# Side products behind the second product, and an expert's split weights kept on chip, in a fused attention and mixture-of-experts kernel

## The chip, the core and the metric

The kernel runs on one core of a Trainium2 chip. TensorE (PE) multiplies, VectorE (DVE), ScalarE (ACT) and GpSimd (POOL) work elementwise, SyncE (SP) issues the transfers between main memory and the chip's buffers. Each engine runs its own instructions strictly in the order in which they stand, and engines wait for each other by semaphores. The metric is the device time of one execution in microseconds.

## The reference

Eight batches of eight heads go through an attention with 32 memory slots; its output, 4608 rows of 512, goes through four experts whose results are summed with normalised weights.

```python
a = exp(phi - max(phi)); a = a / (sum(a) + 1e-9)          # over 576 positions
k_m, v_m = a^T k, a^T v                                   # 32 slots per head
scores = q k_m^T / 8
attn = softmax(scores)                                    # over the 32 slots
x = attn v_m                                              # 4608 x 512 after the transpose
out = 0
for e in range(4):
    h = max(x @ w1[e], 0)                                 # 512 -> 1024
    out += p[:, e:e + 1] * (h @ w2[e])                    # 1024 -> 512
```

## The kernel before

**Numbers in two halves.** Most float32 operands are written as a rounded high part (an ACT copy to a narrower form) and the remainder (a DVE subtraction), and a product is three matmuls: high by high, high by low, low by high. `split` (L149) is that pair of instructions.

**Folding the attention into the expert.** x is never made. For each expert, v_m is multiplied with w1 once (`vw_mm`, L398), which gives a small matrix `vw`, and the softmax weights `AT` are multiplied with `vw`.

**Steps.** The batches are taken in four pairs, with four experts each; a pair and an expert make 32 steps, 512 steps in all: two batches (`odd`), two halves of their columns, and eight blocks j of 128 hidden units. For a step s there are

- the **first product** `first_mm(s)` (L449): six matmuls over 256 or 320 columns into a PSUM bank, tile `p1`;
- `first_hi` (L462, ACT) and `first_lo` (L477, DVE): the split of max(p1, 0) into `h` (and, where 320 columns are done, `hm`);
- the **second product** `second(s)` (L487): six or nine matmuls over 512 columns that add into the banks `p2`; at j = 7 DVE adds them to the output (L513, L515).

The first product runs AHEAD = 2 steps before its second product. PSUM has eight banks: four for `p2`, and four (`pm`) that `p1` shares with all other products. A new tile in `pm` waits until the bank's last reader is done.

**Side work.** Everything that prepares later steps is side work: splitting weights (`plan_w1`, `plan_w2`), the attention of the next batches (`plan_att`), and the products v_m by w1. The last come in two sorts: for the first pair of batches with all of w1 split anew (`plan_vw`: L401 to L403, read by ACT at L413 and DVE at L419), for later ones from split halves that the first pair stored in main memory (`keep_w1`, L142) and that are loaded again (`plan_vw_heads`: L708 splits nothing, it converts what was loaded; L712 multiplies; L720 copies out; L730 moves rows; L766, L770 and L774 add and split them). A planner (`schedule`, L600) assigns each such operation to a step; the side products are those on PE: L401 to L403, L712, the attention's L265 and L268, L1028, L1163 and L857.

**Order inside a step.** From step 18 on (`MANUAL`) `run_step` (L1235) writes the order out. On PE it is: first product of step s + 2, side products, second product of step s. On DVE the step's side operations are cut in two (`cut`, L1226): those that fit a limit of 2300 (a planner's cost, 290 + 2.42 per column; nothing at j = 0) and wait for no other engine of the same step go ahead of `first_lo`, the others behind it. On ACT a limit of 1400 does the same around `first_hi`.

**Steps 0 to 17** are given by tables (`UNITS_1`, `W1_1`, `VW_1`, `REST_0`) and ordered by a scheduler. Batch 0 needs the first expert's w1 first. It is split as eight tiles, in the head of the kernel and in step 1. In steps 10 to 13 `W1_1` has the same four pieces of w1 loaded and split once more, for batch 1, and `unit_w1(..., True)` stores each of these tiles in main memory as it is made. `new_w1` (L136) hands out six buffers in turn: two named `w1`, four named `rows`.

```python
        n = w1n[0] % (2 + RB)
        w1n[0] += 1
        tag = {"tag": "w1", "bufs": 2} if n < 2 else {"tag": "rows", "bufs": RB}
```

Of the kernel before, what the change touches and what calls it, by code (L numbers as in the profile page):

```python
# [10 lines left out]
F32R = mybir.dt.float32r  # L11
# [7 lines left out]
P = 128  # L19
# [4 lines left out]
NJ = F // P  # L24
# [15 lines left out]
RB = 4  # L40
# [5 lines left out]
STEADY = tuple(range(0, 26))  # L46

UNITS_1 = (1, 5, 5, 6, 5, 6, 8, 9, 10, 11, 11, 12, 17, 13, 13, 20)
W1_1 = (10, 10, 12, 13)
VW_1 = (11, 12, 12, 13, 15, 15, 16, 17)  # L50

REST_0 = (2, 1, 6, 6, 1, 1, 1, 1, 5, 1, 2, 1, 2)
# [3 lines left out]
def body(ctx: ExitStack, tc: tile.TileContext, qm, qt, qh, kv, kvt, phi, phn, prob, w1, w2, out):  # L56
    nc = tc.nc
    pool = lambda name, **k: ctx.enter_context(tc.tile_pool(name=name, bufs=1, **k))
    const, wp, work, att = pool("const"), pool("wp"), pool("work"), pool("att")
# [63 lines left out]
    def take_key(key):  # L123
        assert order[count[1]] == key and count[1] in staged, (key, count)
        raws[key] = staged.pop(count[1])
        count[1] += 1

    def free_key(key):
        del raws[key]
        released.add(numbers[key])  # L130
        stage_released()


    w1t, w2t, w1n = {}, {}, [0]

    def new_w1():  # L136
        n = w1n[0] % (2 + RB)
        w1n[0] += 1
        tag = {"tag": "w1", "bufs": 2} if n < 2 else {"tag": "rows", "bufs": RB}
        return wp.tile([P, 2, 512], F32R, name="w1", **tag)  # L140

    def keep_w1(e, fh, hp):  # L142
        for i in range(2):
            nc.sync.dma_start(
                kept[e, fh, hp][i].rearrange("(s r) f -> r s f", s=2),
                w1t[fh, hp][64 * i:64 * i + 64].bitcast(F32),
            )
# [5 lines left out]
    def split_w1(raw, fh, hp, eng):  # L153
        t = new_w1()
        split(t, raw[:, hp % 2, :], eng)
        w1t[fh, hp] = t

    def unit_w1(k, e, fh, g, keep=False):
        def emit(raw):
            for i in range(2):  # L160
                split_w1(raw, fh, 2 * g + i, nc.vector)
                if keep:
                    keep_w1(e, fh, 2 * g + i)
        return ("w1", e, fh, g), emit

    def unit_w2(k, e, j2, eng=nc.vector):
# [269 lines left out]
    def vw_unit(k, e, fh, hp, odds, tag):  # L436
        vw_out(vw_mm(k, fh, hp, tag), k * E + e, fh, hp, odds)
# [4 lines left out]
    def where(s):  # L442
        k, s = divmod(s, PAIR)
        e, s = divmod(s, STEPS)
        odd, s = divmod(s, 2 * NJ)
        half, j = divmod(s, NJ)
        return k, e, odd, half, j

    def first_mm(s):  # L449
        k, e, odd, half, j = where(s)  # L450
        at_t = st["AT", 2 * k + odd]
        n = HALF[odd][half]
        ps = psum.tile([P, 512], F32, name="p1", tag="pm", bufs=4)[:, :n]
        c, f = slice(HALF[odd][0] * half, HALF[odd][0] * half + n), slice((j % 4) * P, (j % 4) * P + P)
        for g in range(2):
            w = vw[k * E + e, odd, j // 4, g]
            nc.tensor.matmul(ps, w[:, 0, f], at_t[:, g, 0, c], start=g == 0, stop=False)  # L457
            nc.tensor.matmul(ps, w[:, 0, f], at_t[:, g, 1, c], start=False, stop=False)  # L458
            nc.tensor.matmul(ps, w[:, 1, f], at_t[:, g, 0, c], start=False, stop=g == 1)  # L459
        return ps  # L460

    def first_hi(s, ps):  # L462
        _, _, odd, _, j = where(s)
        h = work.tile([P, 2, 2 * P], F32R, name="h", tag="h", bufs=AHEAD + 2)
        parts = [(h, slice(0, 2 * P), slice(0, 2 * P))]
        if ps.shape[1] == WIDE:
            if odd == 0:
                mid[j] = work.tile([P, 2, P], F32R, name="hm", tag="hm", bufs=NJ)
                parts.append((mid[j], slice(0, 64), slice(2 * P, WIDE)))
            else:  # L470
                parts = [(mid[j], slice(64, P), slice(0, 64)), (h, slice(0, 2 * P), slice(64, WIDE))]
        for t, to, at_ in parts:
            nc.scalar.activation(t[:, 0, to], ps[:, at_], AF.Relu)  # L473
        hs[s] = h
        return parts

    def first_lo(ps, parts):  # L477
        for t, to, at_ in parts:
            nc.vector.scalar_tensor_tensor(  # L479
                t[:, 1, to], ps[:, at_], 0.0, t[:, 0, to].bitcast(F32), ALU.max, ALU.subtract  # L480
            )
# [5 lines left out]
    def second(s):  # L487
        k, e, odd, half, j = where(s)
        h = hs.pop(s)
        w = w2t[k, e, j]  # L490
        t0 = (0, 2, 5, 7)[2 * odd + half]
        left = [(t0 + i, h[:, :, i * P:i * P + P]) for i in range(2)]
        if t0 == 5:
            left.append((4, mid[j]))
        for t, x in left:
            if j == 0:
                po[t] = psum.tile([P, DM], F32, name="p2", tag="p2", bufs=4)
            nc.tensor.matmul(po[t], x[:, 0, :], w[:, 0, :], start=j == 0, stop=False)  # L498
            nc.tensor.matmul(po[t], x[:, 0, :], w[:, 1, :], start=False, stop=False)  # L499
            nc.tensor.matmul(po[t], x[:, 1, :], w[:, 0, :], start=False, stop=j == NJ - 1)  # L500
        if j < NJ - 1:
            return
        if e == 0:
            a = work.tile([P, 1024], F32, name="acc", tag="acc", bufs=4)
            for i in range(2):
                acc[k, t0 + i] = a[:, i * DM:i * DM + DM]
            if t0 == 5:
                acc[k, 4] = work.tile([P, DM], F32, name="accm", tag="accm", bufs=1)
        for t, _ in left:
            a, n = acc[k, t], TP * k + t  # L510
            p = pt[:, n, e:e + 1]
            if e == 0:
                nc.vector.tensor_scalar_mul(a, po[t], p)  # L513
            else:
                nc.vector.scalar_tensor_tensor(a, po[t], p, a, ALU.mult, ALU.add)  # L515
            if e == E - 1:
                nc.sync.dma_start(out[n * P:n * P + P, :], a)
# [4 lines left out]
    def at(s, unit):  # L522
        plan[s].append(unit if isinstance(unit, tuple) else (None, unit))
# [9 lines left out]
    def vw_at(s, *a):  # L533
        at(s, lambda: vw_unit(*a, ("pm", 4)))

    rest = [unit_scores(0, t0) for t0 in (2, 4)] + [lambda t0=t0: transposes(0, t0) for t0 in (2, 4)]
    rest += [unit_w1(0, 0, 1, g) for g in range(2)]
    rest += [unit_w2(0, 0, j2) for j2 in range(1, 4)]
    rest += [lambda hp=hp: vw_unit(0, 0, 1, hp, (0,), ("pm", 4)) for hp in range(NP)]
# [5 lines left out]
        at(UNITS_1[1 + i], u)  # L545
    for fh in range(2):
        for g in range(2):
            at(W1_1[2 * fh + g], unit_w1(0, 0, fh, g, True))
            for i in range(2):
                vw_at(VW_1[4 * fh + 2 * g + i], 0, 0, fh, 2 * g + i, (1,))  # L550
    class Op:
        def __init__(self, eng, cost, fn, deps, lo=0, take=None, free=None, late=None):
# [666 lines left out]
    def emit(op):  # L1219
        if op.take is not None:  # L1220
            take_key(op.take)
        op.fn()
        if op.free is not None:
            free_key(op.free)

    def cut(ops_, limit, s):  # L1226
        n = 0
        for op in ops_:
            limit -= op.cost
            if limit < 0 or any(d.step == s and d.eng != op.eng for d, _ in op.deps):  # L1230
                break
            n += 1
        return ops_[:n], ops_[n:]

    def run_step(s):  # L1235
        todo_s, ahead = todo[s], s + AHEAD < LAST
        run_plan(s)
        for op in todo_s["SP"]:
            emit(op)
        if ahead:  # L1240
            ps = first_mm(s + AHEAD)
        before, after = cut(todo_s["ACT"], 1400, s)
        for op in before:
            emit(op)
        if ahead:
            parts = first_hi(s + AHEAD, ps)
        for op in after + todo_s["POOL"]:
            emit(op)
        before, after = cut(todo_s["DVE"], 2300 if s % NJ else 0, s)
        for op in before:  # L1250
            emit(op)
        if ahead:
            first_lo(ps, parts)
        for op in after + todo_s["PE"]:
            emit(op)
        second(s)


    order += early
# [5 lines left out]
    def run_plan(s):  # L1265
        for key, emit in plan[s]:
            if key is None:
                emit()
            else:
                emit(take())  # L1270
# [100 lines left out]
    with tc.manual_schedule():  # L1371
        for s in range(MANUAL, LAST):
            run_step(s)
# [40 lines left out]
```

## Time and profile before

| what | value |
|---|---|
| median of three runs | 1382.89 us (1382.28 to 1385.92) |
| the profiled execution | 1383.84 us, of which the span from first to last instruction is 1382.0 us |
| granted TensorE clock, mean | 0.996 |
| DMA | 211.51 MB in 102974 packets, 50.9% of the 16 engines' span |
| side products on PE after 100 us | L712 192 matmuls, L265 192, L1028 96, L401 to L403 24 each, L268 24, L1163 24, L857 12 |

In the profile's rows "L498 PE MATMUL p<-w,h 128x512" is line 498 on PE, which writes a tile p (p1 and p2 both read "p", since numbers are left out) from w and h. Matmuls overlap: each lasts longer than the distance to the next, so PE is read by the distance from start to start. Unthrottled, that distance is about 0.23 us after a matmul over 512 columns, 0.15 after 320 and 0.12 after 256.

### The profile page before, as it was taken

What the parts mean: (1) busy time and instruction counts of PE and PEld (TensorE: products, weight loads), DVE (VectorE), ACT (ScalarE), POOL (GpSimd) and SP (SyncE); (2) the same over time, 40 slices, a digit from 0 to 9 for tenths busy, and PEclk for the clock granted to TensorE, in tenths of its full rate; (3) what the DMA queues carried; (4) which work ended last, traced back from release to release, by engine and by line L of the source; (5) the groups of instructions that cost most, each with busy time, mean ns of one, the idle gap of its engine ahead of it and who ended that gap; (6) DMA issues with size and microseconds to landing.
All of it is one profiled execution on the core that took longest, in us unless ns stands there. A gap on an engine that the chain in (4) does not pass through costs nothing.

```text
span 1382.0 us, 21847 instructions
## 1 busy us (share of the span) xinstructions
PE 1363.0 (99%) x7444; PEld 1190.2 (86%) x7444; DVE 844.0 (61%) x1859; ACT 739.0 (53%) x1747; POOL 27.5 (2%) x27
## 2 busy tenths in 40 slices
PE   7999999999999999999999999999999999999998
PEld 6888888888888888888888888888888888888887
DVE  7867667577676656666567565665666644444532
ACT  7545555446556556565554656565665644455321
POOL 4300000000000000000000000000000000000000
PEclk9999999999999999999999999999999999999999
DMA  6756254254666556553664657555465545536101
GB/s 238 230 188 231 96 173 148 90 163 126 177 185 190 149 171 182 155 176 90 183 177 125 205 167 195 140 168 159 132 186 153 172 106 163 142 124 165 34 31 38
DMA packets 102974, 211.51 MB, mean 153 GB/s; under 512 B 18256, under 2 KB 18640, under 8 KB 102864
## 3 DMA queue, kind: packets, MB, share of 16 engines
q1 hardware_dynamic: 102864, 210.12, 50.9%
q8 instruction: 59, 0.97, 0.3%
q14 instruction: 51, 0.42, 0.1%
HBM read 133.51 MB, written 26.21 MB: 116 GB/s over the span
## 4 chain that ended last, share of the span: by engine, by line
PE 93%; DVE 2%; ACT 2%; DMA 2%; issue 1%; SPq 0%; POOL 0%; ACTq 0%; DVEq 0%
PE p L499 18%; PE p L498 18%; PE p L500 18%; PE p L457 10%; PE p L459 9%; PE p L458 9%; PE pv L712 3%; PE x L265 2%; PE sT L1028 1%; DMA stage<-w 1%; PE pv L401 1%; PE sc L340 1%; PE pv L402 1%; PE pv L403 1%; ACT w L708 0%
## 5 line engine op out<-in xcount | busy, mean ns | idle before, releaser
L473 ACT ACTIVATE h<-p 128x256 fp32r<-128x256 f32 x512 | 196.3, 384 | 411.5 <-PE p L459 392.1
L479 DVE SCALAR_TENSOR_TENSOR h<-p,h 128x256 fp32r<-128x256 f32 x512 | 215.4, 421 | 310.7 <-ACT h L473 184.5
L498 PE MATMUL p<-w,h 128*128 128x512 f32 x1024 | 404.1, 395 | 0.2 <-ACT h L473 0.2
L499 PE MATMUL p<-w,h 128*128 128x512 f32 x1024 | 403.5, 394 | 0.0
L500 PE MATMUL p<-w,h 128*128 128x512 f32 x1024 | 401.4, 392 | 0.0
L457 PE MATMUL p<-AT,vw 128*128 128x256 f32 (+1 forms) x1024 | 304.8, 298 | 1.5 <-DVE h L479 0.8
L458 PE MATMUL p<-AT,vw 128*128 128x256 f32 (+1 forms) x1024 | 302.7, 296 | 0.6 <-DVE AT L393 0.6
L459 PE MATMUL p<-AT,vw 128*128 128x256 f32 (+1 forms) x1024 | 302.1, 295 | 0.3 <-DVE vw L419 0.3
L500 PEld LDWEIGHTS p<-w,h 128*128 128x128 f32 x1024 | 192.3, 188 | 43.5
L499 PEld LDWEIGHTS p<-w,h 128*128 128x128 f32 x1024 | 192.8, 188 | 28.2 <-DVE w L151 0.4
L457 PEld LDWEIGHTS p<-AT,vw 128*128 128x128 f32 x1024 | 192.7, 188 | 27.1 <-issue 3.3
L498 PEld LDWEIGHTS p<-w,h 128*128 128x128 f32 x1024 | 192.5, 188 | 26.8 <-ACT h L473 0.4
L458 PEld LDWEIGHTS p<-AT,vw 128*128 128x128 f32 x1024 | 193.9, 189 | 21.2 <-DVE AT L393 0.8
L459 PEld LDWEIGHTS p<-AT,vw 128*128 128x128 f32 x1024 | 193.1, 189 | 0.8 <-DVE vw L419 0.5
L479 DVE SCALAR_TENSOR_TENSOR hm<-p,hm 128x64 fp32r<-128x64 f32 x256 | 56.0, 219 | 149.2 <-ACT h L473 148.6
L473 ACT ACTIVATE hm<-p 128x64 fp32r<-128x64 f32 x256 | 56.8, 222 | 149.9 <-PE p L459 149.8
L720 ACT COPY E<-pv 128x512 f32<-128x512 f32 x192 | 111.6, 595 | 18.8 <-DMA rows<-E 14.1
L708 ACT CAST w<-stage 128x1024 fp32r<-128x1024 f32 x96 | 100.7, 1049 | 1.7 <-DMA stage<-w 1.6
L794 DVE TENSOR_TENSOR w<-stage,w 128x512 fp32r<-128x512 f32 x120 | 79.5, 682 | 0.1
L790 ACT CAST w<-stage 128x512 fp32r<-128x512 f32 x120 | 73.3, 616 | 2.5 <-DMA stage<-in_w 2.1
L774 DVE TENSOR_TENSOR vw<-rows,vw 128x512 fp32r<-128x512 f32 x96 | 64.7, 686 | 12.2 <-ACT vw L770 11.4
L515 DVE SCALAR_TENSOR_TENSOR acc<-p,pt,acc 128x512 f32<-128x512 f32 x96 | 67.4, 742 | 5.6 <-PE p L500 5.4
(135 smaller groups left out, 1338.0 us busy)
## 6 DMA issues: line engine op xcount, KB each, us to landing
stage<-w SPq DMA_DIRECT2D x96, 512.0 KB, 4.3
rows<-E SPq DMA_DIRECT2D x768, 64.0 KB, 2.8
stage<-in_w SPq DMA_DIRECT2D x84, 512.0 KB, 4.2
stage<-in_kv SPq DMA_DIRECT2D x32, 512.0 KB, 4.4
w<-w SPq DMA_DIRECT2D x64, 256.0 KB, 4.7
out<-acc SPq DMA_DIRECT2D x32, 256.0 KB, 3.7
stage<-in_qh SPq DMA_DIRECT2D x24, 288.0 KB, 3.2
ph<-in_phi SPq DMA_DIRECT2D x16, 288.0 KB, 4.2
```

Source lines behind the costliest of these rows:

```text
L457: nc.tensor.matmul(ps, w[:, 0, f], at_t[:, g, 0, c], start=g == 0, stop=False)
L458: nc.tensor.matmul(ps, w[:, 0, f], at_t[:, g, 1, c], start=False, stop=False)
L459: nc.tensor.matmul(ps, w[:, 1, f], at_t[:, g, 0, c], start=False, stop=g == 1)
L473: nc.scalar.activation(t[:, 0, to], ps[:, at_], AF.Relu)
L479: nc.vector.scalar_tensor_tensor(t[:, 1, to], ps[:, at_], 0.0, t[:, 0, to].bitcast(F32), ALU.max, ALU.subtract)
L498: nc.tensor.matmul(po[t], x[:, 0, :], w[:, 0, :], start=j == 0, stop=False)
L499: nc.tensor.matmul(po[t], x[:, 0, :], w[:, 1, :], start=False, stop=False)
L500: nc.tensor.matmul(po[t], x[:, 1, :], w[:, 0, :], start=False, stop=j == NJ - 1)
L708: nc.scalar.copy(w, raws[key])
L720: nc.scalar.copy(box["E"][:, i, :], box[i])
L790: nc.scalar.copy(t[:, 0, :], raws[key][:, i, :])
L794: nc.vector.tensor_sub(t[:, 1, :], raws[key][:, i, :], t[:, 0, :].bitcast(F32))
```

## The change

Three edits. (1) In `run_step` the side products are written behind the second product instead of ahead of it. (2) The limit of side work that DVE does ahead of `first_lo` falls from 2300 to 1000, so that no operation over 512 columns fits any more. (3) The first expert's eight split tiles are kept until batch 1 has used them: tiles 6 and 7 get buffers of the tag `vw1`, the second load and split in steps 10 to 13 go, and the eight stores are named for steps 9 to 16, one each. The planner's assignment of work to steps is the same before and after.

```diff
-W1_1 = (10, 10, 12, 13)
+KEEP_1 = (9, 10, 11, 12, 13, 14, 15, 16)
...
     def new_w1():
-        n = w1n[0] % (2 + RB)
+        n = w1n[0]
         w1n[0] += 1
+
+        if 2 + RB <= n < 8:
+            return att.tile([P, 2, 512], F32R, name="w1", tag="vw1", bufs=6)
+        n = (n if n < 8 else n - 8) % (2 + RB)
         tag = {"tag": "w1", "bufs": 2} if n < 2 else {"tag": "rows", "bufs": RB}
...
-    def unit_w1(k, e, fh, g, keep=False):
+    def unit_w1(k, e, fh, g):
         def emit(raw):
             for i in range(2):
                 split_w1(raw, fh, 2 * g + i, nc.vector)
-                if keep:
-                    keep_w1(e, fh, 2 * g + i)
...
-            at(W1_1[2 * fh + g], unit_w1(0, 0, fh, g, True))
             for i in range(2):
+                at(KEEP_1[4 * fh + 2 * g + i], lambda fh=fh, hp=2 * g + i: keep_w1(0, fh, hp))
                 vw_at(VW_1[4 * fh + 2 * g + i], 0, 0, fh, 2 * g + i, (1,))
...
-        before, after = cut(todo_s["DVE"], 2300 if s % NJ else 0, s)
+        before, after = cut(todo_s["DVE"], 1000 if s % NJ else 0, s)
...
-        for op in after + todo_s["PE"]:
+        for op in after:
             emit(op)
         second(s)
+        for op in todo_s["PE"]:
+            emit(op)
```

How the order of instructions moves is shown at three places; lines of the changed kernel stand two or four higher.

ACT, late in the attention of batch 1 (kvs are split keys and values, xs the copied sums of a pair of heads, p_ a first product, w_988 and w_993 two of the tiles split anew). Before:

```order
L253 CAST kvs<-stage 128x512 x2
L473 ACTIVATE h<-p_809 128x256
L473 ACTIVATE hm<-p_809 128x64
L150 CAST w_988<-stage 128x512
L150 CAST w_993<-stage 128x512
L277 COPY xs<-x 128x256 x2
L295 COPY kvT_76<-kvp 64x2x2x32
```

and now:

```order
L255 CAST kvs<-stage 128x512 x2
L475 ACTIVATE h<-p_811 128x256
L475 ACTIVATE hm<-p_811 128x64
L279 COPY xs<-x 128x256 x2
L297 COPY kvT_76<-kvp 64x2x2x32
```

The two casts of w that stood ahead of the copies xs are gone.

SP, from the end of the kernel's head on (w_000_82 and so on are the stored tiles in main memory, in_w, in_qm, in_kvt and in_kv are inputs). Before:

```order
L107 DMA stage<-in_w 128x1024
L107 DMA stage<-in_qm 128x1024
L107 DMA stage<-in_w 128x1024
L107 DMA stage<-in_kvt 128x1024
L107 DMA stage<-in_kv 128x1024 x4
L107 DMA stage<-in_w 128x1024 x2
L844 DMA ph<-in_phi 128x576 x2
L107 DMA stage<-in_qm 128x1024
L144 DMA w_000_82<-w_860 64x2x512
```

and now:

```order
L107 DMA stage<-in_w 128x1024
L148 DMA w_000_82<-w_280 64x2x512 x2
L148 DMA w_001_83<-w_314 64x2x512 x2
L148 DMA w_002_84<-w_321 64x2x512 x2
L107 DMA stage<-in_qm 128x1024
L107 DMA stage<-in_w 128x1024
L107 DMA stage<-in_kvt 128x1024
L107 DMA stage<-in_kv 128x1024 x4
L107 DMA stage<-in_qm 128x1024
L148 DMA w_003_85<-w_324 64x2x512 x2
```

The first three tiles are stored ahead of the loads for batch 1, whatever step the table names, and two loads of w behind the four of kv are gone.

PE in one step with a side product, at 579.7 us of the trace (p_6433 is a first product, p_6318 a second one; its other matmuls, of the same form, are left out at the end). Before:

```order
L459 MATMUL p_6433<-AT,vw 128x256
L712 MATMUL pv<-w_6412,vt 128x512
L498 MATMUL p_6318<-w_6256,h 128x512
L499 MATMUL p_6318<-w_6256,h 128x512
L500 MATMUL p_6318<-w_6256,h 128x512
```

and now:

```order
L461 MATMUL p_6401<-AT,vw 128x256
L500 MATMUL p_6276<-w_6224,h 128x512
L501 MATMUL p_6276<-w_6224,h 128x512
L502 MATMUL p_6276<-w_6224,h 128x512
L500 MATMUL p_6280<-w_6224,h 128x512
L501 MATMUL p_6280<-w_6224,h 128x512
L502 MATMUL p_6280<-w_6224,h 128x512
L714 MATMUL pv<-w_6380,vt 128x512
```

The product pv has moved behind all six matmuls of the second product.

DVE in the step at 515 us of the trace (rows is the sum for a `vw`, h and hm the split of a first product). Before:

```order
L766 TENSOR_TENSOR rows<-rows 128x512
L479 SCALAR_TENSOR_TENSOR h<-p_5698,h 128x256
L479 SCALAR_TENSOR_TENSOR hm<-p_5698,hm 128x64
L766 TENSOR_TENSOR rows<-rows 128x512
L479 SCALAR_TENSOR_TENSOR h<-p_5730,h 128x256
```

and now:

```order
L481 SCALAR_TENSOR_TENSOR h<-p_5666,h 128x256
L481 SCALAR_TENSOR_TENSOR hm<-p_5666,hm 128x64
L768 TENSOR_TENSOR rows<-rows 128x512 x2
L481 SCALAR_TENSOR_TENSOR h<-p_5698,h 128x256
```

Both additions now stand behind the split of the first product.

## The prediction

> **What bounds the kernel now.** I read the page first, its busy times and its chain:
>
> ```profile
> span 1382.0 us, 21847 instructions
> PE 1363.0 (99%) x7444; PEld 1190.2 (86%) x7444; DVE 844.0 (61%) x1859; ACT 739.0 (53%) x1747; POOL 27.5 (2%) x27
> PE 93%; DVE 2%; ACT 2%; DMA 2%; issue 1%; SPq 0%; POOL 0%; ACTq 0%; DVEq 0%
> ```
>
> PE is the bound, and the change takes no matmul away. It can only remove or add time in which PE waits. So the second view is that of PE's own waits, of which these rows bear on the change (who waited for whom: us in all, times, longest):
>
> ```profile
> PE kvp L285 <- ACT xs L277: 2.5, 1, 2.5
> PE pv L712 <- DVE xs L1155: 1.7, 2, 1.0
> PE pv L401 <- DVE vw L419: 1.3, 4, 0.4
> PE p L457 <- DVE h L479: 0.8, 2, 0.6
> PE x L265 <- DVE xs L1155: 0.6, 1, 0.6
> PE p L457 <- DVE hm L479: 0.3, 1, 0.3
> PE p L457 <- ACT E L720: 0.2, 1, 0.2
> ```
>
> The first row is one wait in steps 0 to 17, where edit 3 works. The pv and x rows are seven waits of side products, which edit 1 moves. The p rows are four waits of first products, in reach of edit 2. The sum is small: 7.4 us, and what hides behind overlapping matmuls comes on top.
>
> **Edit 3, the opening.** PE's timeline around the longest wait, and the windows around it:
>
> ```profile
> 66.88 0.28 PE L268 MATMUL x<-tl,a 128*128 128x256 f32 x1
> 67.47 0.40 PE L500 MATMUL p<-w,h 128*128 128x512 f32 x1
> 70.38 0.96 PE L285 MATMUL kvp<-ident,xs 128*128 128x128 f32 x4 [2.51 <-ACT xs L277]
> ...
> 67.00:70.60 3.60, 1.09 (x7) 0.58 (x5) 1.03 (x2) 1.68 (x4) 0.00 (x0) 1.00 1.00 281
> 70.60:74.00 3.40, 3.40 (x13) 3.08 (x12) 1.62 (x7) 1.14 (x5) 0.00 (x0) 0.51 1.00 387
> ```
>
> PE idles 2.51 us, and in the 3.40 us behind it the granted clock (the last number but two) is 0.51. ACT's timeline tells why it idled:
>
> ```profile
> 64.96 0.22 ACT L473 ACTIVATE hm<-p 128x64 fp32r<-128x64 f32 x1
> 68.92 1.14 ACT L150 CAST w<-stage 128x512 fp32r<-128x512 f32 x2 [3.73 <-DMA stage<-in_w]
> 69.96 0.64 ACT L277 COPY xs<-x 128x256 f32<-128x256 f32 x2
> ```
>
> The two casts belong to the second split of w1. They wait 3.73 us for a load, and the copies xs, whose input x was done at 67.16 (66.88 + 0.28), stand behind them. Without the casts ACT is free at 65.18, so the copies run from about 67.2 to 67.85; PE's own matmul ends at 67.87. I leave 0.2 us of idle: **2.3 us** gained. The half clock in 70.60:74.00 costs half of 3.4 us. With a gap of 0.2 instead of 2.5 us I expect it not to come: **1.7 us** gained.
>
> The rest of what goes lies beside a PE that runs without a gap:
>
> ```profile
> L150 ACT CAST w<-stage x22: 611/618/647, 17.7 to 81.9; 128x512 fp32r<-128x512 f32 x22
> L151 DVE TENSOR_TENSOR w<-stage,w x19: 671/685/1777, 21.6 to 86.7; 128x512 fp32r<-128x512 f32 x19
> L144 SPq DMA_DIRECT2D w<-w x64: 575/720/2327, 59.2 to 307.1; - x64
> ...
> 16.52 0.37 SPq L107 DMA_DIRECT2D stage<-in_w  x1
> 33.95 0.33 SPq L107 DMA_DIRECT2D stage<-in_qm  x1
> ```
>
> Of each operation the medians are 0.618, 0.685 and 0.720 us (the middle numbers). Eight casts (4.9 us of ACT), eight subtractions (5.5 us of DVE) and four loads go; beyond the wait above I count them as nothing. The sixteen store issues stay, and six of them move ahead of the loads for batch 1 on SP. Their tiles are split in the kernel's head, and at that place SP issues nothing from 16.9 to 33.95 us, so six issues of 0.72, 4.3 us, fit. Without that gap they would put the loads, and batch 1, 4.3 us back.
>
> One loss: the reordered opening puts a long DVE operation ahead of a split h near 48 us.
>
> ```profile
> 47.56 0.42 DVE L479 SCALAR_TENSOR_TENSOR h<-p,h 128x256 fp32r<-128x256 f32 x1
> 48.00 0.74 DVE L185 TENSOR_REDUCE nm<-ph 128x1 f32<-128x576 f32 x1
> 48.20 0.71 PE L500 MATMUL p<-w,h 128*128 128x512 f32 x2
> ```
>
> In the new order the maximum of L185 comes ahead of that h, which then ends about 0.6 us later, at 48.6; PE wanted it at 48.20. I charge **0.4 us**; bounds 0 and 0.74. Edit 3 in all: 2.3 + 1.7 - 0.4 = 3.6 us gained.
>
> **Edit 1, side products behind the second product.** One of the seven waits, on PE and DVE:
>
> ```profile
> 580.18 0.28 PE L458 MATMUL p<-AT,vw 128*128 128x256 f32 x1
> 580.30 0.28 PE L459 MATMUL p<-AT,vw 128*128 128x256 f32 x1
> 580.41 0.98 DVE L1155 SCALAR_TENSOR_TENSOR xs<-x,rz,xt 64x256 f32<-64x256 f32 x2 [1.49 <-ACT xt L1145]
> 581.42 0.42 DVE L479 SCALAR_TENSOR_TENSOR h<-p,h 128x256 fp32r<-128x256 f32 x1
> 581.53 0.47 PE L712 MATMUL pv<-w,vt 128*128 128x512 f32 x1 [0.95 <-DVE xs L1155]
> 581.84 0.40 PE L498 MATMUL p<-w,h 128*128 128x512 f32 x1
> ...
> 132.00 0.28 PE L459 MATMUL p<-AT,vw 128*128 128x256 f32 x1
> 132.53 0.47 PE L401 MATMUL pv<-w,vt 128*128 128x512 f32 x1 [0.26 <-DVE vw L419]
> ```
>
> pv reuses the bank that DVE is still reading at L1155. From start to start it takes 1.23 us (580.30 to 581.53) where neighbours take 0.12: the wait costs 1.11 us, 0.16 more than the idle time of the row, and the matmul behind it (581.84) starts 0.31 instead of 0.23 us later, another 0.08. So seven waits of 3.6 us idle (1.7 + 1.3 + 0.6) cost 3.6 + 7 x 0.24 = 5.3 us. Ahead of pv will now stand six matmuls of the second product, 6 x 0.23 = 1.4 us, more than the longest excess of 1.11. DVE's L1155 itself may be put off by work that edit 2 moves ahead of it, one operation of 0.68; the waits at L401 (0.4 us) stand that too. I count all **5.3 us** as gained; bounds 2.7 (half) and 5.3.
>
> Does the second product then wait for h? At 581.42 DVE makes the h of the first product that has just run, which is used two steps on, while PE starts a second product whose h is two steps old. The move takes at most one step's side products off this distance, a kv product of nine matmuls at 0.12, 1.1 us. It hides entirely: nothing charged.
>
> What is late next? Behind a side product now stands the next first product, and whatever still holds the side product up holds that one up too. A side product's own bank is filled one second product later, and may have to be read before a first product two steps on. Of the operations that read it, most stand behind `first_hi` and `first_lo` of the next step in any case, so their times hardly move; I charge the rest with edit 2.
>
> **Edit 2, DVE's limit.** A case on DVE, and the group of the first product's first line after 100 us (busy, mean | idle before it):
>
> ```profile
> 514.87 0.69 DVE L766 TENSOR_TENSOR rows<-rows 128x512 f32<-128x512 f32 x1 [1.07 <-DMA rows<-E]
> 515.48 0.42 DVE L479 SCALAR_TENSOR_TENSOR h<-p,h 128x256 fp32r<-128x256 f32 x1
> 515.82 0.21 DVE L479 SCALAR_TENSOR_TENSOR hm<-p,hm 128x64 fp32r<-128x64 f32 x1
> ...
> L457 PE MATMUL p<-AT,vw 128*128 128x320 f32 (+1 forms) x984 | 292.3, 297 | 1.5 <-DVE h L479 0.8 <-DVE hm L479 0.3 <-ACT E L720 0.2
> ```
>
> DVE waits 1.07 us for moved rows, adds them, and only then splits h; the next first product needs that bank. Now the split comes first. The waits are 1.5 us idle, with 0.24 hidden at each of the four listed 2.5 us. Some of them end on ACT or at j = 0, where the limit was nothing already; I take **1.8 us** gained, bounds 0 and 2.5.
>
> The price: a DVE side operation ends up to 0.7 us later, and ACT operations that read it may stand ahead of `first_hi`. No row shows it; the nearest are the most frequent side product and the copy that reads it:
>
> ```profile
> L712 PE MATMUL pv<-w,vt 128*128 128x512 f32 x192 | 64.9, 394 | 1.8 <-DVE xs L1155 1.7
> L720 ACT COPY E<-pv 128x512 f32<-128x512 f32 x192 | 111.6, 595 | 18.8 <-DMA rows<-E 14.1
> ```
>
> From below it is 0; from above, half of the 192 tiles each hold PE up by a copy of 0.595 us, 57 us. In the trace one first product waits for such a copy, 0.2 us, so I take a value near the lower end, **1.0 us** lost.
>
> **The sum.** 3.6 + 5.3 + 1.8 - 1.0 = 9.7 us. The profiled execution took 1383.84 us (span 1382.0 and 1.84 around it), 0.95 above the median of 1382.89. So its counterpart is 1374.1 and the median **1373.2 us**.
>
> [...]
>
> **Rivals.**
> - **Only the opening gains.** Each removed wait of edits 1 and 2 comes back one product later. For it: four banks are still shared, and side tiles are read no earlier. Against: 1.4 us of cover exceed each wait. 3.6 us, 1379.3. Chance 0.11.
> - **Only the order gains.** The transposes kvp at 70.38 find another late input, such as SP's moved stores delaying batch 1, and the gap and the half clock remain. Against: x was done at 67.16. 9.7 - 3.6 = 6.1 us, 1376.8. Chance 0.12.
> - **The half clock stays** though the gap goes, from another cause: 8.0 us, 1374.9. Chance 0.06.
> - **Slower: late banks.** A side tile filled at a step's end is not read when the next first product wants a bank, and PE waits for one L720 copy, 0.595 us. Of 192 such tiles, 17 use up the gain of 9.7 us: the point is one in eleven. One in five, 38, costs 22.6 us, 12.9 more than the gain: 1395.8. For it: PE already waits for L720 once. Against: only once, for 0.2 us. Chance 0.05.
>
> **How the numbers follow.** The forecast has 0.66. Its own bounds are -11.8 us (no price, no loss at 48 us, all p waits gone) to -7.1 (half of edit 1's gain), and the three runs lie from 0.6 below to 3.0 above their median. The range reaches from 1370.0 over the half clock and the order-only case to 1378.5; it leaves out the opening-only and the late-bank case, 0.16. A measurement of this kernel tells 0.3%, 4.1 us, from no change. Faster: forecast, order-only and half clock, 0.84. Same: opening-only, 0.11. Slower: 0.05.
>
> **What would show it.** PE's waits: the row kvp after xs falls from 2.5 to under 0.5, and no 0.5 clock appears after 20 us. The rows pv and x after DVE are gone, as are most after h. Wrong would be a new row of p (first products) after ACT E, DVE vw or h worth several us, or a second product that waits for h.

## The result, and the profile after

| what | before | changed |
|---|---|---|
| median of 6 runs | 1383.69 us (1382.28 to 1386.03) | 1374.48 us (1372.99 to 1375.94) |
| ratio of the times, 95% interval | | 0.993 [0.9917, 0.9944] |
| profiled execution | 1383.84 us | 1374.13 us |

The change made the kernel 0.7% faster. The forecast was 1373.2 us (1370.0 to 1378.5), and for the counterpart of the profiled execution 1374.1 us. The page of the changed kernel: span, busy times, chain.

```profile
span 1372.4 us, 21779 instructions
...
PE 1356.9 (99%) x7444; PEld 1186.9 (86%) x7444; DVE 834.0 (61%) x1851; ACT 742.7 (54%) x1739; POOL 27.0 (2%) x27
...
PE 95%; DMA 2%; DVE 1%; ACT 1%; SPq 0%; issue 0%; ACTq 0%; DVEq 0%
```

PE has the same 7444 matmuls and is still the bound; DVE and ACT have eight instructions less each. Its waits now (who waited for whom: us in all, times, longest):

```profile
PE x L267 <- DVE a L224: 2.7, 1, 2.7
...
PE p L459 <- DVE h L481: 1.6, 1, 1.6
PE tpa L218 <- DVE ph L203: 1.6, 3, 0.6
PE p L459 <- ACT E L722: 1.1, 2, 0.5
...
PE p L502 <- DVE nm L190: 0.2, 1, 0.2
```

The rows kvp after xs, pv after DVE and x after xs are gone, as forecast. The largest row, x L267 with 2.7 us, lies at 11 us in the head of the kernel; it comes and goes with the execution (2.8 us with edit 1 alone, 0.9 in a second execution of the changed kernel) and is no effect of the change. Rows of first products were announced as a sign of error if they were worth several us. Two are there, smaller than that: one first product (p L459) waits 1.6 us for h, and two wait 1.1 us together for the copy E.

To see where time goes or comes from, I compared the start of the same matmul of the second product in two traces (those over 512 columns, 3456 in each) at four places. Differences to the kernel before, in us; e1 to e12 are the experiments below:

| kernel | up to 33 us (the head) | 33 to 60 | 60 to 83 | 83 to the end | windows at half clock: head, near 70 us, later |
|---|---|---|---|---|---|
| before | 0 | 0 | 0 | 0 | 2, 1, 0 |
| changed | -0.66 | +0.73 | -4.23 | -5.41 | 1, 0, 0 |
| changed, again (e5) | -0.75 | +0.77 | -4.23 | -5.90 | 2, 0, 0 |
| edit 3 alone (e1) | -1.63 | +0.74 | -4.21 | +1.58 | 0, 0, 0 |
| edit 1 alone (e2) | -0.31 | +0.44 | -2.37 | -5.22 | 1, 0, 0 |
| edit 2 alone (e3) | -1.04 | +0.36 | -1.74 | -0.08 | 1, 0, 0 |
| edits 1 and 2 (e4) | -1.74 | +0.06 | -0.05 | -3.72 | 0, 1, 0 |
| edits 1 and 3 (e6) | -0.84 | +0.76 | -4.22 | -3.86 | 2, 0, 0 |
| changed, moves on two queues (e9) | -1.20 | +0.78 | -4.22 | -7.89 | 1, 0, 0 |

**The opening.** Windows around the place where PE had idled 2.51 us (PE, PEld, DVE, ACT, POOL busy, then granted clock, DMA share, GB/s), and the copies xs on ACT's timeline:

```profile
62.60:66.20 3.60, 3.60 (x26) 3.33 (x25) 1.30 (x5) 1.99 (x6) 2.31 (x2) 1.00 0.69 197
66.20:69.60 3.40, 3.40 (x23) 2.85 (x22) 0.76 (x3) 1.14 (x4) 0.23 (x1) 1.00 0.65 190
69.60:73.00 3.40, 3.40 (x26) 3.19 (x25) 2.23 (x7) 1.10 (x5) 0.00 (x0) 1.00 0.95 321
```
```profile
67.31 0.65 ACT L279 COPY xs<-x 128x256 f32<-128x256 f32 x2 [2.20 <-PE x L270]
```

PE is busy throughout at full clock. ACT now waits 2.20 us for PE, not PE for ACT.

**A side product behind the second product**, the counterpart of the place at 580 us:

```profile
574.10 0.28 PE L461 MATMUL p<-AT,vw 128*128 128x256 f32 x1
574.21 0.98 DVE L1157 SCALAR_TENSOR_TENSOR xs<-x,rz,xt 64x256 f32<-64x256 f32 x2 [1.49 <-ACT xt L1147]
574.22 0.40 PE L500 MATMUL p<-w,h 128*128 128x512 f32 x1
...
575.38 0.39 PE L502 MATMUL p<-w,h 128*128 128x512 f32 x1
575.61 0.39 PE L714 MATMUL pv<-w,vt 128*128 128x512 f32 x1
575.84 0.30 PE L459 MATMUL p<-AT,vw 128*128 128x320 f32 x1
```

DVE reads the bank until 575.19 (574.21 + 0.98), just as late after the first product as before, but the second product covers it: pv starts at 575.61 without a wait, and the next first product 0.23 us behind it.

**The new wait for h**, at the step where before the wait was 0.2 us. Timelines of SP, ACT, DVE and PE in the changed kernel:

```profile
501.35 0.38 SPq L107 DMA_DIRECT2D stage<-w  x1
501.77 6.61 SPq L732 DMA_DIRECT2D rows<-E  x8
508.48 0.53 SPq L107 DMA_DIRECT2D stage<-w  x1
...
512.94 1.05 ACT L710 CAST w<-stage 128x1024 fp32r<-128x1024 f32 x1 [1.42 <-DMA stage<-w]
...
513.43 0.39 PE L502 MATMUL p<-w,h 128*128 128x512 f32 x1
...
513.90 0.61 ACT L772 CAST vw<-rows 128x512 fp32r<-128x512 f32 x1
514.41 0.22 ACT L475 ACTIVATE hm<-p 128x64 fp32r<-128x64 f32 x1
...
514.94 0.23 DVE L481 SCALAR_TENSOR_TENSOR hm<-p,hm 128x64 fp32r<-128x64 f32 x1 [2.82 <-ACT h L475]
...
515.64 0.39 PE L459 MATMUL p<-AT,vw 128*128 128x320 f32 x1 [1.59 <-DVE h L481]
```

and SP and PE in the kernel before:

```profile
507.10 0.38 SPq L107 DMA_DIRECT2D stage<-w  x1
507.52 6.83 SPq L730 DMA_DIRECT2D rows<-E  x8
514.45 0.53 SPq L107 DMA_DIRECT2D stage<-w  x1
...
521.05 0.39 PE L500 MATMUL p<-w,h 128*128 128x512 f32 x1
...
521.65 0.39 PE L457 MATMUL p<-AT,vw 128*128 128x320 f32 x1 [0.21 <-DVE h L479]
```

Read from the end: PE waits for DVE's h, DVE for ACT's h, ACT for its cast of w, the cast for a load that SP issued at 508.48. SP issued it behind eight moves of rows that took 6.61 us. The load is 5.97 us earlier than before (514.45 to 508.48), while the last matmul of PE's second product there is 7.62 us earlier (521.05 to 513.43). PE gained on the way, SP did not, and PE waits there for most of the difference. SP itself stood still for 1.8 us within those moves (2.0 us in the kernel before):

```profile
SPq L732 <- DMA stage<-w: 1.8, 1, 1.8
```

It waited for the load issued at 501.35 to land, which is the transfer that it had issued eight before. In the trace of the changed kernel all 32 issues of SP that waited for a transfer waited for the one issued exactly eight before, in that of before all 34. (SP's separate semaphore waits, ahead of loads and at the end, were ended 15 times by a transfer issued one to four before, 11 times in before.) The reason stands in the program: SP's 1137 issues use eight semaphores strictly in turn, and nearly all of them (1063) carry a wait for their own semaphore or have it just ahead, that is for the landing of the transfer eight before. So the trace shows a wait that the program holds; a limit of the queue itself it doesn't show.

### The profile page after: what moved, and what is told of

Its sections match the earlier page's. It is cut to its first block, busy times and chain, and to the rows that moved or that the text cites. A ratio compares the mean times of both kernels' runs of the same rounds, so it can differ in the third digit from the quotient of the medians.

```text
span 1372.4 us, 21779 instructions
## 1 busy us (share of the span) xinstructions
PE 1356.9 (99%) x7444; PEld 1186.9 (86%) x7444; DVE 834.0 (61%) x1851; ACT 742.7 (54%) x1739; POOL 27.0 (2%) x27
## 4 chain that ended last, share of the span: by engine, by line
PE 95%; DMA 2%; DVE 1%; ACT 1%; SPq 0%; issue 0%; ACTq 0%; DVEq 0%
PE p L501 19%; PE p L502 19%; PE p L500 19%; PE p L459 10%; PE p L461 10%; PE p L460 10%; PE pv L714 3%; PE x L267 2%; PE sT L1030 1%; DMA stage<-w 1%; PE sc L342 1%; PE pv L403 1%; PE pv L405 1%; PE pv L404 1%; DMA stage<-in_kv 0%
## 5 line engine op out<-in xcount | busy, mean ns | idle before, releaser
L502 PE MATMUL p<-w,h 128*128 128x512 f32 x1024 | 401.9, 393 | 0.2 <-DVE nm L190 0.2
L459 PE MATMUL p<-AT,vw 128*128 128x256 f32 (+1 forms) x1024 | 305.7, 299 | 3.0 <-DVE h L481 1.6
L502 PEld LDWEIGHTS p<-w,h 128*128 128x128 f32 x1024 | 192.2, 188 | 43.3 <-DVE nm L190 0.5
L459 PEld LDWEIGHTS p<-AT,vw 128*128 128x128 f32 x1024 | 192.4, 188 | 24.5 <-issue 3.0
```

## The experiments

Times are compared with runs of the kernel before on the same chip. The first four take the change apart.

**Edit 3 alone (e1).** `W1_1` goes, `KEEP_1` and the new `new_w1` come; `run_step` is as before.

> Edit 3 alone (the tiles stay, the stores are spread; order and limit as before). If the three edits add up, the opening's gain is the one that the trace of the changed kernel shows up to 95 us, 4.2 us: about 1379.5 us against 1383.7, the wait of 2.5 us for xs and the half clock at 70 us both gone. If the opening only gains together with the new order of later steps, it would be within 1 us of before. If the second split was not the cause of the half clock, the gap goes and a stretch at 0.5 stays near 70 us: about 1381.2.

Measured: 1380.64 us against 1382.57, ratio 0.9987 [0.9979, 0.9996]. The trace has the opening's gain as expected (-4.21 us between 60 and 83 us), and so the opening doesn't need the other edits. The time shows only half of it. Behind 83 us this execution lost 1.58 us in waits that the trace of before has smaller: 1.2 us for hm at 511 us (0.2 at that step before), 0.4 for E at 844, 0.3 for E at 944. ACT's casts and copies E ahead of them wait again for transfers that SP issued. And the half clock near 70 us, which the comparison with one trace of before counts in full, isn't there in every execution (below).

**Edit 1 alone (e2).**

```diff
-        for op in after + todo_s["PE"]:
+        for op in after:
             emit(op)
         second(s)
+        for op in todo_s["PE"]:
+            emit(op)
```

> Edit 1 alone (side products behind the second product; the limit stays 2300, w1 is split twice). Theory of the sum: the seven listed waits of side products (4.9 us from start to start with the one at 689 us) go, and the new waits of first products (3.1 us in the changed kernel) come: about 1.5 to 4.5 us faster, 1379 to 1382. Rival (the edits need each other): with operations over 512 columns still ahead of the split h, the first product that now stands right behind the side product finds its bank unread, the waits move to first products and nothing is gained: 1383 to 1385.

Measured: 1378.38 us against 1382.57, ratio 0.9971 [0.9958, 0.9983], near the upper end of the theory's 1.5 to 4.5 us; behind 83 us the trace gained 5.22 us, since the new waits of first products are smaller than in the changed kernel (0.8 us at 510 us is the largest). PE's waits:

```profile
PE kvp L285 <- ACT xs L277: 1.7, 1, 1.7
PE p L457 <- DVE hm L479: 1.2, 2, 0.8
PE p L457 <- DVE h L479: 0.8, 2, 0.6
```

No row of a side product is left. The move needs neither the limit nor the opening; the rival falls. The wait for xs is 1.7 us here, and no half clock followed.

**Edit 2 alone (e3)**, the limit 1000 in place of 2300.

> Edit 2 alone (DVE's limit 1000; side products ahead of the second product, w1 split twice). Theory of the sum as predicted: 1.8 us of waits for h go and 1.0 us of late banks come: 0.8 us faster, 1382.9. Rival: operations over 512 columns that read a side product's bank come later while the side products come no later, so the waits of side products at the seven places grow by up to 0.7 us each: up to 5 us slower, 1388.7.

Measured: 1383.1 us against 1382.57, ratio 1.0001 [0.9991, 1.0011]; -0.08 us behind 83 us. Neither side was right about the sizes: waits for h (0.8) and hm (0.3) went, waits for E grew instead:

```profile
PE pv L712 <- DVE xs L1155: 1.7, 2, 1.0
PE p L457 <- ACT E L720: 1.5, 2, 1.0
```

The waits of side products did not grow, which speaks against the rival.

**Edits 1 and 2 without 3 (e4).**

> Edits 1 and 2 without edit 3. Theory of the sum: what the trace of the changed kernel gained behind 95 us, 5.4 us: 1378.3. Its waits of 0.5 to 1.7 us at first products (near 350, 518 and 1082 us here) come back at the same steps. Rival: these waits come from the earlier start that edit 3 gave, then they are absent here and the gain is 7 to 8 us: 1376.

Measured: 1378.69 us against 1382.57, ratio 0.9963 [0.9949, 0.9977]; -3.72 us behind 83 us. The waits come back at 350, 516 and 1081 us, so edit 3 doesn't make them. One more is new: 1.4 us for E at 843 us. Adding the limit to edit 1 changed nothing that the times can tell (1378.38 and 1378.69).

**The changed kernel again (e5), and with the limit at 2300 (e6)**, which is edits 1 and 3.

> The changed kernel once more, beside the two that follow. Theory of the sum: 1373 to 1376 us. Its profile shows how far the opening and the waits at first products differ from one execution to the next: if they hang on the state of the transfers, the waits near 350, 514 and 1077 us and those for E change size by 0.5 us or more, or appear at other steps; if they come from the order alone, they are the same within 0.05 us.

> The changed kernel with DVE's limit at 2300 again (edits 1 and 3 without 2). If the limit gives what the prediction said (0.8 us net), it is 0.8 us slower than the changed kernel. From the first four kernels I now expect the limit to give nothing: behind 95 us edit 1 alone gained 5.2 us, both together 3.7 to 5.4 us; so the two are the same within 1.5 us, and the waits of first products for h (0.8 us at 1020 us, 0.5 us at 1085) are there, that for E at 1077 is not.

Measured: 1374.02 and 1375.51 us against 1382.49; ratios 0.9936 [0.9923, 0.995] and 0.9949 [0.9934, 0.9964]. The changed kernel waited 1.9 us at 513 us here, 1.6 in its first profile; not at all at 347 us, 0.5 in the first; and 0.5 us near 1077 in both. So the wait at 347 us hangs on the state of the transfers. The one at 513 changed by 0.3 us, between the two marks of the expectation; the experiments on POOL below decide it. The one at 1077 hangs on the order: 0.54 us of it stand in every trace with edit 2 that was taken up to here (e3 and e4 too), and none in those without. With the limit at 2300 the waits for h and hm at 1014 and 1079 us are there (0.6 and 0.3), that for E at 1077 is not. What the limit is worth stays open within about 2 us: nothing alone, nothing on top of edit 1, 1.5 us on top of edits 1 and 3, where the intervals overlap.

**The loads on POOL (e7).**

```diff
-            nc.sync.dma_start(t, src)
+            (nc.gpsimd if order[i][0] == "heads" else nc.sync).dma_start(t, src)
```

> The changed kernel with the 96 loads of stored w1 tiles (stage<-w) issued by POOL instead of SP. Theory: the waits near 347 and 514 us come from SP's queue, where loads stand behind moves of rows that take 0.6 us each: the cast of w at 513 us then no longer waits 1.4 us for its load, the first product behind it waits less than 0.4 us in place of 1.6, and E's copies are released earlier; 1 to 3 us faster than the changed kernel. Rival: the transfers themselves (traffic) are late, not their issue: the cast waits as before and the time is the same within 1 us, or slower, if an issue on POOL lands later than one on SP.

Measured: 1376.24 us against 1382.49, ratio 0.9956 [0.9942, 0.997]: 2.2 us slower than the changed kernel beside it. Both sides were half right. The wait at 513 us is gone, as the theory wanted. But E's copies wait longer:

```profile
PE p L459 <- ACT E L722: 2.4, 2, 1.9
```

At 839 us PE idles 1.9 us for E, with a window at half clock behind it. The loads were taken out of SP's queue, the moves on which E waits were not: ACT's copy E waits 4.1 us for a move ahead of that place.

**Gaps of PE and the clock (e8).** POOL copies a split h onto itself 4 to 20 times at eleven steps.

```diff
             first_lo(ps, parts)
+        for _ in range(HOLD.get(s, 0)):
+            x = hs[s + AHEAD][:, 0, :]
+            nc.gpsimd.tensor_copy(x, x)
```

> The changed kernel in which POOL copies a split h onto itself 4 to 20 times at eleven steps (60, 92, 124, ... 380), so that the second product two steps on waits; the values stay the same. It measures what an idle gap of PE does to the granted clock. Theory 1: the clock is set by windows of about 3.4 us that run free; a gap under 2 us never halves it, one of 2.3 to 2.6 us does by chance of where it lies in its window, one over about 5 us always, and each half-rate stretch lasts 3.4 us or a multiple. Theory 2: a fixed length of a gap decides (2.5 us or more halves the clock each time, less never). Theory 3: gaps have nothing to do with it, and the half-rate stretches stand elsewhere. The time is longer by the gaps' sum, some 20 to 60 us.

Measured: 1432.08 us in one execution, within what was expected. Two of its gaps, and what follows them (granted clock is the last number but two):

```profile
388.83:389.95 1.12, 0.00 (x1) 0.00 (x0) 0.95 (x3) 1.12 (x4) 1.00 (x2) 1.00 0.85 150
390.00:396.00 6.00, 6.00 (x34) 5.23 (x35) 4.21 (x8) 2.12 (x5) 0.00 (x0) 1.00 0.33 112
472.13:474.78 2.65, 0.00 (x1) 0.00 (x0) 2.40 (x5) 1.00 (x2) 2.41 (x4) 1.00 0.52 155
475.30:478.60 3.30, 3.30 (x12) 2.83 (x12) 0.00 (x0) 0.00 (x0) 0.00 (x0) 0.50 0.59 173
```

Every stretch at half clock that ends within a trace lasts 3.413, 6.827 or 10.240 us (the last behind e8's gap at 1100 us), and within one trace their starts lie whole multiples of 3.4133 us apart (in the trace of before 9.198, 70.638 and 1381.356). From the span's start the grid lies differently in two executions (9.198 us in before, 11.914 in the changed kernel, 2.716 apart), so in these traces it doesn't hang on the start. With that grid, a gap in the steps can be cut into windows of 3.4133 us; most of those over 1.5 us in all kernels:

| kernel, place | gap of PE | largest idle share of a window | half clock after it |
|---|---|---|---|
| e2, 68 us | 1.67 us | 0.40 | no |
| e3, 67 us | 2.32 us | 0.37 | no |
| e5, 513 us | 1.87 us | 0.37 | no |
| changed, 514 us | 1.59 us | 0.46 | no |
| e4, 517 us | 1.64 us | 0.48 | no |
| e6, 508 us | 1.66 us | 0.49 | no |
| e7, 839 us | 1.91 us | 0.56 | yes, 1 window |
| e10, 514 us | 2.13 us | 0.57 | yes, 1 |
| e4, 66 us | 2.41 us | 0.71 | yes, 1 |
| before, 68 us | 2.51 us | 0.74 | yes, 1 |
| e8, 472 us | 2.65 us | 0.78 | yes, 1 |
| e8, 562 us | 3.11 us | 0.62 | yes, 2 |
| e8, 1100 us | 7.75 us | 1.00 | yes, 3 |

A gap of 2.32 us that two windows share left the clock alone, one of 1.91 us within one window halved it. Theory 1 fits these gaps: after a share of 0.56 or more came half clock, after one of 0.49 or less it did not; its bound that a gap under 2 us never halves the clock was wrong (1.91 us did). Theories 2 and 3 fall. What sets the clock no trace shows, only when it changed. These shares are of windows at full clock in the steps. A window already at half clock was followed by another one after less idle time: after 0.29 to 0.39 in five cases of e8, among them the second window of the gap of 3.11 us, and not after 0.06; in the head of the kernel before after 0.37 (at 9.198 us) and not after 0.05. In the head, where PE has many short gaps, the shares don't sort as cleanly: one of 0.40 was followed by half clock (e5), one of 0.46 was not (e1).

**Half of the moves on POOL (e9).**

```diff
-                    nc.sync.dma_start(t[to:to + M, s, :], box["E"][at_:at_ + M, i, :])
+                    (nc.gpsimd if odd else nc.sync).dma_start(t[to:to + M, s, :], box["E"][at_:at_ + M, i, :])
```

> The changed kernel with half of the moves of rows (odd = 1, 384 of 768) issued by POOL; the loads stay on SP. Theory: the waits of first products near 347, 513 and 841 us come from SP, which issues a move each 0.6 us and stops when the transfer issued eight before has not landed; with half of the moves elsewhere the loads and E's release come earlier, the waits at 513 (1.6 to 1.9 us) and 347 or 841 go, that at 1077 (ACT's order) stays: 1371 to 1372.5 us, 2 us faster than the changed kernel. Rival: the transfers' own traffic is late, as when POOL issued the loads; then E's copies wait as long or longer and the time is 1374 to 1377.

Measured: 1371.66 us (1371.24 to 1372.06) against 1381.79, ratio 0.9919 [0.9906, 0.9932], as the theory had it. It beats both kernels: each of its five runs lies below each of the changed kernel's twelve (1372.99 at least), though the two intervals overlap. On the same chip e10 and e11 below, whose times don't differ from the changed kernel's, have no run under 1372.45 us. SP and ACT at the place of the wait at 513 us:

```profile
500.91 0.38 SPq L107 DMA_DIRECT2D stage<-w  x1
...
509.07 1.05 ACT L710 CAST w<-stage 128x1024 fp32r<-128x1024 f32 x1
```

The load is issued 7.57 us earlier than in the changed kernel (508.48 to 500.91), PE is 1.25 us earlier there; the cast doesn't wait, and no first product waits for h. ACT's waits for transfers behind 100 us, in the kernel before, the changed one and this one:

```profile
ACT E L720 <- DMA rows<-E: 14.1, 9, 4.7
...
ACT w L708 <- DMA stage<-w: 1.6, 2, 1.1
```
```profile
ACT E L722 <- DMA rows<-E: 24.7, 13, 4.5
...
ACT w L710 <- DMA stage<-w: 4.2, 6, 1.4
```
```profile
ACT E L722 <- DMA rows<-E: 4.6, 4, 1.8
...
ACT w L710 <- DMA stage<-w: 0.7, 1, 0.7
```

The change raised both rows; the second queue takes them below those of before.

**The stores at their old steps (e10).**

```diff
-KEEP_1 = (9, 10, 11, 12, 13, 14, 15, 16)
+KEEP_1 = (10, 10, 10, 10, 12, 12, 13, 13)
```

> The changed kernel with the eight stores of w1 at the steps where they stood before (10, 10, 10, 10, 12, 12, 13, 13) in place of 9 to 16. Theory: the stores only need SP's time and nobody waits for them in the opening, so the spreading is worth nothing: the same as the changed kernel within 1 us, the opening up to 95 us within 0.3 us by its profile. Rival: the stores in a heap put the loads of batch 1 back by up to 4 issues of 0.7 us, and the wait for xs or for a split comes back: 1 to 3 us slower.

Measured: 1373.59 us against 1381.79, ratio 0.9931 [0.9917, 0.9944]; 33 to 60 us +0.77, 60 to 83 us -4.24, as with the stores spread. Spreading is worth nothing here; the gain of edit 3 is the second split that goes.

**The casts behind h (e11).**

```diff
-            if limit < 0 or any(d.step == s and d.eng != op.eng for d, _ in op.deps):
+            if limit < 0 or op.take is not None or any(d.step == s and d.eng != op.eng for d, _ in op.deps):
```

> The changed kernel in which ACT does the casts that read a freshly loaded buffer, and what follows them in the step's list, behind the split h (first_hi) instead of ahead of it. Theory: at 513 us the first product waits since the cast of w waits 1.4 us for its load ahead of h; with the cast behind h the wait there falls below 0.4 us, and the kernel gains 1 to 1.6 us: 1372.5 to 1373.5. Rival: the casts, the copies E and the split vw that follow come up to 1 us later throughout, side products wait for w (PE pv after ACT w) and banks are read later: 1375 to 1380.

Measured: 1374.56 us against 1381.79, ratio 0.9938 [0.9924, 0.9952], no different from the changed kernel; the wait at 514 us is 1.4 us. My theory fell at this point, and ACT's timeline says why:

```profile
510.99 0.40 ACT L475 ACTIVATE h<-p 128x256 fp32r<-128x256 f32 x1
...
513.08 1.05 ACT L710 CAST w<-stage 128x1024 fp32r<-128x1024 f32 x1 [1.56 <-DMA stage<-w]
```

The cast stood behind the h of its own step already. It is the next step's h that it holds up, whatever its place within the step. What helps is an earlier load, not another place of the cast.

**The kernel before with half of its moves on POOL (e12).**

> The kernel before with half of the moves of rows (odd = 1) issued by POOL. On the changed kernel that took 2.4 us away (1374.0 to 1371.7). Theory: SP's queue became a bound through the change, which made PE 1 us earlier at 498 us but not SP; in the kernel before its waits behind SP are only those at 521 (0.4 us), 417 and 770 us, so this gains 0.4 to 1.0 us: 1381.5 to 1382.2 against 1382.5, and the seven waits of side products stay as they were. Rival: SP's queue costs the kernel before as much as the changed one, then it gains 2 to 2.5 us (about 1380), and the change has given nothing back there.

Measured: 1382.26 us against 1384.06, ratio 0.9994 [0.9982, 1.0007]; behind 83 us -1.21 us. The ratio stands for 0.8 us, the two medians for 1.8. The first and the trace are nearer to the theory's 0.4 to 1.0 than to the rival's 2 to 2.5, but the interval reaches 2.5 us (0.9982), so these runs don't exclude the rival. The waits of side products stayed:

```profile
PE kvp L285 <- ACT xs L277: 3.6, 1, 3.6
...
PE pv L712 <- DVE xs L1155: 1.7, 2, 1.0
PE pv L401 <- DVE vw L419: 1.3, 4, 0.4
```

The wait for xs took 3.6 us in this execution, the largest of all.

## Why the prediction was right

The time lies 1.3 us above the forecast, and the sum for the profiled execution (9.7 us) is what was measured (9.7 us); between the medians it is 9.2 us. That the profiled execution agrees to 0.1 us is luck: up to 83 us it gained 0.6 us more than predicted, which is the scatter of the head, and behind it 0.7 us less.

The times of the experiments say the same less sharply. By the medians, edit 3 was worth 1.9 us alone (0.6 to 2.9 by its interval, less than the 3.6 forecast) and 2.8 on top of edit 1; edit 1 was worth 4.2 us alone and about 5 on top of edit 3, where 5.3 were forecast. Whether edit 3 is worth more beside the others than alone stays open within the intervals.

- **The wait for xs, 2.3 us.** Right. Between 60 and 83 us 4.23 us went in each kernel with edit 3, where 2.3 + 1.7 = 4.0 were forecast. The six stores that moved ahead took SP 6.6 us instead of the 4.3 reckoned, and still fit in front of the next load at 33.28 us.
- **The half clock, 1.7 us.** Right in its cause, too large as a term. In the steps it followed a gap where 0.56 or more of a window was idle (0.74 in the kernel before), and not where 0.49 or less was. The executions without edit 3 had gaps of 1.7, 2.3, 2.4, 2.5 and 3.6 us, and half clock after three of them. With half a window, a value between those two, taken as the limit, either part of the gap of 2.51 us must stay under 1.71 us to go free, which 0.91 of 3.41 positions do, 27%. So a typical run holds about 1.2 us of it, an estimate from these numbers, where the profiled execution held all 1.7.
- **The loss at 48 us, 0.4 us.** Too small, and partly at another place: 0.73 us between 33 and 60. The split h that comes behind the maximum cost 0.2 (the row p L502, where the view names the small operation nm that ended just behind it); 0.6 more is a transpose (tpa) that waits for the norm of L203 on DVE, in the reordered opening. That norm took 1.19 us here and 0.52 before (1.2 in e1, e5 and e9, 0.5 in e2): with edit 3 it runs beside POOL's L256 for 0.9 us, without it for 0.2. That POOL slows it fits these traces, but no experiment separates the two. The prediction looked at one operation that moved and not at its neighbours.
- **The head.** Not foreseen: -0.66 us up to 33 us, where the trace of before has two windows at half clock and that of the changed kernel one. Other executions have none to two, at offsets from -1.80 to +0.40 us. The offsets show no order by edits: -1.80 and -1.74 stand for kernels without edit 3, -1.63 for one with it. So it is scatter, not an effect of the change; that it comes from where the windows fall is likely, but not shown.
- **The seven waits, 5.3 us.** Right. They are gone in every kernel with edit 1, and edit 1 alone gained 5.22 us behind 83 us. The cover of six matmuls was enough, and behind 60 us no second product waits for h in the changed kernel.
- **DVE's limit, 1.8 gained and 1.0 lost.** Not confirmed in size. The waits for h and hm of 0.6 and 0.3 us (at 1022 and 1087 us) did go, and a wait for E of 0.5 us at 1077 came, as priced. But the limit alone gave nothing.
- **"What is late next?"** Here a step failed. The prediction looked at the banks and at DVE. The largest wait that was left grew at 521 us, which edit 2 was to remove: from 0.2 to 1.6 us. It hangs on ACT's cast, on its load, and on SP's queue of moves, in which the 1.0 us that PE gained at 498 us was lost. That this is the cause is shown by two experiments: with the loads or half of the moves on another queue the wait is gone, and with the latter the kernel is 2 us faster.

The rivals: "only the opening" falls by the second and fourth experiment, in which the order gains without edit 3, and "only the order" by the first, in which the opening gains without the order. "The half clock stays" falls by the changed kernel's windows. "Late banks" was there in kind, 1.1 us for E, far from the 9.7 us at which it would have decided.

## What to carry to other kernels

A wait of one engine on another's reading of a shared bank was hidden here by putting other matmuls of the same engine between, 1.4 us of them (6 x 0.23) against 1.11 us. A removed wait can make the next queue late, as here, and the question is which one did not speed up with the engine. Look at queues of transfer issues as at engines: here eight moves behind each other held up the next load, and a second queue was worth 2 us. The single gap of 2.51 us cost its length and, in the execution compared, 1.7 us of half clock on top (a gap of 1.67 us in e2 cost none), and the six runs of the kernel before lie 3.75 us apart, so compare several executions before a difference of 1 or 2 us is put down to an edit.

## What the runs showed of the hardware

- In the trace of the kernel before, the granted clock fell to 0.50 at 9.198, 70.638 and 1381.356 us, 18 and 384 times 3.4133 us apart. Among the gaps listed above, all in the steps, a window of that length at full clock with 0.56 or more of PE idle (e7 the least) was followed by one at 0.50, one with up to 0.49 (e6) was not.
- In this program an issue of SP waits where the transfer that it issued eight before has not landed: 34 of 34 issues that waited for a transfer in the kernel before, 32 of 32 in the changed one, by the program's own semaphores. In the changed kernel a move of 64 KB took 0.59 us to issue (median of 768), eight took 5.02 us from 509.64 on; the load of 512 KB issued at 501.35 landed only after 6.5 us and cost SP 1.8 us.
- With half of the moves on each (e9), POOL issued one in 0.50 us (SP four in 2.42 us at 498.03), and it landed as soon (medians 3.5 and 3.9 us for the two halves). On one queue, in the changed kernel, the median was 2.7 us, so the gain of two queues lies in the earlier issue, not in a faster transfer:

```profile
L732 POOL DMA_DIRECT2D rows<-E x384 | 189.7, 499 | 1012.5 <-ACT E L722 818.8
...
rows<-E POOLq DMA_DIRECT2D x384, 64.0 KB, 3.5
rows<-E SPq DMA_DIRECT2D x384, 64.0 KB, 3.9
```
